# Re-ordering the tail of a fused transformer block: output projection, LayerNorm statistics and pending down tiles around the last attention group

## Chip, cores, metric

One core of one Trainium2 chip. The metric is the device time of one execution in microseconds (us), the median of several runs; a change of less than 2% counts as "same". Each run carries the granted TensorE clock; all runs used here were classed as fast. Each run is one core, so there is no second die to compare with.

## The reference, cut to what matters

```python
# S = 2048 tokens, D = 640, H = 32 heads of Dh = 20, one K/V head, Df = 1536, bf16
def _A_ref(x, wq, wk, wv, wo):                 # multi-query attention
    q = (x @ wq).reshape(B, S, H, Dh).transpose(0, 2, 1, 3)
    k, v = x @ wk, x @ wv
    p = softmax(einsum("bhqd,bkd->bhqk", q, k) * Dh ** -0.5)
    return einsum("bhqk,bkd->bhqd", p, v) ... @ wo
def _B_ref(x, w_gate, w_up, w_down):           # gated FFN
    return (gelu(x @ w_gate) * (x @ w_up)) @ w_down
h  = x + _A_ref(layernorm(x), ...)
h2 = h + _B_ref(layernorm(h), ...)
```

## The kernel before

The tokens are handled in four chunks of 512. In each chunk there are eight groups of four heads ("gi", 32 in all), and each group needs 16 steps of score matmul, exp on ScalarE, and value matmul. While attention of chunk 1, 2, 3 runs, TensorE's spare time takes the output projection, LayerNorm and FFN of the chunk before. So after the last exp a *tail* is left that nothing can hide: finish the last group, project chunk 3, normalise it, transpose it by DMA, its whole FFN (12 units), its four down tiles, and four *pending* down tiles of chunk 2. (A down tile is the last product of the FFN for 128 tokens: 12 matmuls of 512 columns, 12 of 128. `bank(n)` is one of eight accumulators in PSUM; TensorE fills it, and another engine has to read it before it is used again.)

Every operation is put in the queue of its engine in program order and waits for named events. In the traces here an operation late in a queue starts only behind the earlier ones of its engine, which is what this case is about. (An example, shown below: the matmuls for the first pending tile's first add end at 1033.2 us, and the add starts at 1040.08, behind the whole normalise.)

The last group is finished in a chain across VectorE ("dve") and TensorE ("pe"):

```python
def plan_group_copy(qc, g):       # after the last value matmul; bank(6) holds the sums
    plan.op("dve", ... tensor_copy(opvT32, bank(6)), mark=("ocopy", gi))
    plan.op("dve", ... tensor_copy(opvT16, opvT32), mark=("ocopy16", gi))
def piece_L(qc, g):               # broadcast each head's softmax sum over its rows
    plan.op("pe",  ... matmul(bank(7), bcast, opvT16), mark=("L", gi))
    plan.op("dve", ... tensor_copy(rL_sb, bank(7)), mark=("Lcopy", gi))
    plan.op("dve", ... reciprocal(rL_sb, rL_sb), mark=("recip", gi))
    plan.op("dve", ... onT[:, qc % 2, g, :] = opvT32 * rL_sb, mark=("onorm", gi))
```

The projection of a 128-token tile adds up eight head groups `g`; seven of them have been ready long before the last. The tail of the kernel before (shortened):

```python
piece_L(NQC - 1, NG - 1)()
def tail_wo(qc, qt):                       # two bank pairs (0,1), (2,3) in turn
    waits = [("onorm", gidx(qc, NG - 1)), ...] + S_FREE      # all eight groups wait
    plan.op("pe", lo_fn, wait=waits, mark=("wo_lo", t))      # 8 matmuls, columns 0..511
    plan.op("pe", hi_fn, wait=..., mark=("wo_hi", t))        # 8 matmuls, columns 512..639
    plan.op("dve", ... xh_sb += lo_b, mark=("attn_lo", t))
    plan.op("dve", ... xh_sb += hi_b, mark=("attn_hi", t))
for qt in range(TPC):
    tail_wo(NQC - 1, qt)
plan_ln2_chunk(NQC - 1)                    # all statistics, small chain, normalise, transposes
...
for tc in pending_down:                    # four tiles, bank pairs (4,5), (6,7) in turn
    for qt in range(TPC):
        ...                                # 12 + 12 matmuls, then fin_lo, fin_hi on dve
        if qt >= 2: waits6.append(("fin_lo", t - 2))
# then the FFN loop; its unit 0 waits for the last pending tiles' adds
```

In the FFN loop, per unit: `gu` (10 matmuls), `gs` (ScalarE copy), `sq`, `z` (VectorE), `th` (ScalarE tanh), `hg`, `hh` (VectorE): steps of gelu(gate) times up, and `hh` is the unit's result, which the down tiles read. VectorE's order in one iteration is hg and hh of unit i-2, z of i-1, sq of i.

The softmax here doesn't subtract the row's maximum and nothing guards it: scores larger than these inputs give would overflow.

## Time and profile before

| | before |
|---|---|
| median of 5 runs | 1108.76 us (1107.53 to 1110.01) |
| span of the profiled run | 1106.2 us |
| ScalarE busy | 89%, of it 950.9 us exp |
| tail, from the end of the last exp | 94.5 us |

From the page of the kernel before: span, line of busy times (busy us, share of the span, instructions), the chain by engine, and the costliest group of instructions.

```profile
span 1106.2 us, 13023 instructions
...
PE 755.6 (68%) x5424; PEld 203.1 (18%) x5508; DVE 461.5 (42%) x741; ACT 984.7 (89%) x1124; POOL 15.6 (1%) x20
...
ACT 63%; issue 17%; DVE 12%; PE 6%; DMA 1%; SPq 0%; POOL 0%; POOLq 0%
...
L485 ACT ACTIVATE scratch_a<-ps 128x1024 bf16<-128x1024 f32 x1024 | 950.9, 1138 | 23.8 <-PE ps L472 22.8
```

ScalarE's exp is the attention's limit and most of the chain. The change leaves all of that alone.

The timeline of the kernel before, in the tail: start us, length us, engine, line, operation, result<-inputs, shapes; in brackets the idle time of the engine just before and who ended it.

```profile
1012.42 0.69 DVE L519 COPY opvT<-ps 128x512 f32<-128x512 f32 x1 [19.09 <-PE ps L491]
...
1019.14 3.55 PE L978 MATMUL ps<-wo_pad,onT 128*128 128x512 bf16 x8 [6.77 <-DVE onT L541]
...
1022.72 0.69 DVE L993 TENSOR_TENSOR xh_sb<-xh_sb,ps 128x512 bf16<-128x512 bf16 x1 [3.64 <-PE ps L978]
...
1030.43 2.75 PE L786 MATMUL ps<-wd_sb,hhT 128*128 128x512 bf16 x12
...
1034.72 0.21 DVE L286 BATCH_NORM_AGGREGATE mv<-stats 128x2 f32<-128x12 f32 x1
...
1038.04 5.16 SPq L337 DMA_TRANSPOSE xnT<-xn_tmp  x4
...
1039.78 0.39 DVE L329 TENSOR_SCALAR xn_tmp<-xn_tmp,ln_r 128x640 bf16<-128x640 bf16 x1
1040.08 0.68 DVE L803 TENSOR_TENSOR xh_sb<-xh_sb,ps 128x512 bf16<-128x512 bf16 x1
...
1040.82 5.30 PE L786 MATMUL ps<-wd_sb,hhT 128*128 128x512 bf16 x12 [3.24 <-DVE xh_sb L803]
...
1051.04 0.78 PEld L682 LDWEIGHTS ps<-xnT,wg_sb 128*128 128x128 bf16 x5 [0.61 <-issue]
...
1087.29 0.69 DVE L741 SCALAR_TENSOR_TENSOR hhT<-g_th,ps 128x512 bf16<-128x512 bf16 x1
...
1088.03 4.10 PE L786 MATMUL ps<-wd_sb,hhT 128*128 128x512 bf16 x12 [5.80 <-DVE hhT L741]
```

How to read it. The last group's first copy starts at 1012.42; I use that moment as zero below, because all that comes before is attention. Until the last multiply is done TensorE has only the one broadcast matmul `L` (its record is missing, so the 6.77 us of idle time include it); it starts the projection at 1019.14. The last statistic starts at 1034.72, the transposes start at 1038.04 and take 5.16 us. The third pending tile starts at 1040.82, released by the first pending tile's add at 1040.08, which had stood behind the normalise (last step 1039.78) though its matmuls, started at 1030.43, had long ended. The third tile's 12 wide matmuls take 5.30 us, where the first tile's took 2.75. The first gate matmul's weights are loaded at 1051.04.

The granted clock (next to last but two) in stretches of the kernel before; columns: stretch, its length, then busy time and instructions of TensorE, its weight loads, VectorE, ScalarE, GpSimd, then clock, DMA share, GB/s.

```profile
1019.14:1021.00 1.86, 1.86 (x5) 0.73 (x6) 0.00 (x0) 0.00 (x0) 0.00 (x0) 0.50 0.00 0
1023.00:1026.00 3.00, 2.94 (x25) 1.55 (x23) 1.56 (x4) 0.00 (x0) 0.00 (x0) 1.00 0.00 0
...
1041.00:1044.00 3.00, 3.00 (x8) 1.06 (x7) 0.75 (x2) 0.00 (x0) 0.00 (x0) 0.50 0.68 132
1088.00:1090.00 2.00, 1.97 (x5) 0.73 (x6) 0.00 (x0) 0.00 (x0) 0.00 (x0) 0.50 0.00 0
```

Half clock after each long wait: at the projection's start, at the third pending tile, at the first of the last down tiles.

### The profile page before, as it was taken

To read this page: it belongs to the slowest core of one execution; us is meant where nothing else is said; L and a number is where in the kernel's file an instruction comes from. 1 tells how busy PE (TensorE), PEld (TensorE's weight loads), DVE (VectorE), ACT (ScalarE), POOL (GpSimd) and SP (SyncE) were. 2 spreads that over 40 slices of the span, in tenths; PEclk is the share of its full clock that TensorE was granted. 3 is DMA by queue.
4 is the path that set the end of the run, shared out by engine and by line. 5 is a ranking of instruction groups with operands and counts; after the bars stand their busy time and mean duration, and the time that the engine had idled before them with its cause. 6 is when DMAs were issued, how large, how long until landed. Compare 5 with 4: busy or idle time off the path is not lost.

```text
span 1106.2 us, 13023 instructions
## 1 busy us (share of the span) xinstructions
PE 755.6 (68%) x5424; PEld 203.1 (18%) x5508; DVE 461.5 (42%) x741; ACT 984.7 (89%) x1124; POOL 15.6 (1%) x20
## 2 busy tenths in 40 slices
PE   1677666666667776666876777667776776765886
PEld 0111111111121111111222111111221111111433
DVE  7433222111254666411224456661224356642574
ACT  3799999999899999999999999999999999995041
POOL 3000000000000000000000000000000000000000
PEclk9699655555899999755999999985999699985899
DMA  6360000000000000000000100000000100000100
GB/s 168 77 221 1 1 1 1 1 1 0 1 12 12 1 1 1 1 1 1 13 12 1 25 1 1 1 1 1 19 7 1 25 1 1 1 1 0 42 7 24
DMA packets 31819, 18.92 MB, mean 17 GB/s; under 512 B 23568, under 2 KB 30480, under 8 KB 31760
## 3 DMA queue, kind: packets, MB, share of 16 engines
q1 hardware_dynamic: 31760, 18.08, 6.0%
q8 instruction: 43, 0.70, 0.3%
q14 instruction: 16, 0.13, 0.0%
HBM read 10.21 MB, written 2.62 MB: 12 GB/s over the span
## 4 chain that ended last, share of the span: by engine, by line
ACT 63%; issue 17%; DVE 12%; PE 6%; DMA 1%; SPq 0%; POOL 0%; POOLq 0%
ACT scratch_a L485 61%; DVE rL_sb L537 3%; PE ps L786 2%; ACT g_th L728 2%; PE ps L682 1%; DVE hhT L741 1%; DVE g_th L733 1%; DVE g_sq L722 1%; DVE stats L281 1%; PE ps L491 1%; DVE stats L276 1%; PE ps L472 1%; DVE xn_tmp L329 1%; DMA xh_sb<-in_A_x_dram 1%; DVE xn_tmp L321 1%
## 5 line engine op out<-in xcount | busy, mean ns | idle before, releaser
L485 ACT ACTIVATE scratch_a<-ps 128x1024 bf16<-128x1024 f32 x1024 | 950.9, 1138 | 23.8 <-PE ps L472 22.8
L491 PE MATMUL ps<-scratch_a,v_ext 128*32 128x512 bf16 x2048 | 244.9, 469 | 194.1 <-ACT scratch_a L485 187.5
L472 PE MATMUL ps<-qT,kT 32*128 32x512 bf16 x2048 | 242.6, 464 | 85.9 <-ACT scratch_a L485 79.1
L491 PEld LDWEIGHTS ps<-scratch_a,v_ext 128*32 128x32 bf16 x2048 | 54.0, 96 | 383.4 <-ACT scratch_a L485 377.0
L519 DVE COPY opvT<-ps 128x512 f32<-128x512 f32 x32 | 22.1, 691 | 243.7 <-PE ps L491 243.7
L472 PEld LDWEIGHTS ps<-qT,kT 32*128 32x128 bf16 x2048 | 53.3, 94 | 313.1 <-ACT scratch_a L485 299.0
L537 DVE RECIPROCAL rL_sb<-rL_sb 128x512 f32<-128x512 f32 x32 | 107.3, 3353 | 1.1
L682 PE MATMUL ps<-xnT,wu_sb 128*128 128x512 bf16 x228 | 67.1, 399 | 7.7 <-DVE g_gs L710 5.7
L682 PE MATMUL ps<-xnT,wg_sb 128*128 128x512 bf16 x220 | 63.4, 390 | 9.4 <-DVE hhT L741 4.0
L786 PE MATMUL ps<-wd_sb,hhT 128*128 128x512 bf16 x185 | 52.2, 413 | 9.8 <-DVE hhT L741 5.8
L712 ACT ACTIVATE g_gs<-ps 128x512 bf16<-128x512 f32 x12 | 7.2, 597 | 54.8 <-PE ps L682 54.8
L775 DVE CAST g_us<-ps 128x512 bf16<-128x512 f32 x36 | 24.9, 690 | 74.4 <-PE ps L682 74.4
L535 DVE COPY rL_sb<-ps 128x512 f32<-128x512 f32 x32 | 22.0, 689 | 60.2 <-PE ps L491 53.2
L423 DVE CAST qT<-ps 128x512 bf16<-128x512 f32 x31 | 21.4, 690 | 56.7 <-PE ps L601 56.7
L710 DVE CAST g_gs<-ps 128x512 bf16<-128x512 f32 x36 | 24.8, 689 | 40.7 <-PE ps L682 40.7
L728 ACT ACTIVATE g_th<-g_sq 128x512 bf16<-128x512 bf16 x48 | 34.7, 724 | 5.4 <-DVE g_sq L722 5.4
L733 DVE SCALAR_TENSOR_TENSOR g_th<-g_th,g_gs 128x512 bf16<-128x512 bf16 x48 | 32.9, 686 | 6.8 <-ACT g_th L728 6.7
L722 DVE SCALAR_TENSOR_TENSOR g_sq<-g_sq,g_gs 128x512 bf16<-128x512 bf16 x48 | 32.7, 682 | 0.0
L626 PE MATMUL ps<-wo_pad,onT 128*128 128x512 bf16 x88 | 28.2, 395 | 4.9 <-DVE onT L541 3.6
L803 DVE TENSOR_TENSOR xh_sb<-xh_sb,ps 128x512 bf16<-128x512 bf16 x16 | 11.0, 685 | 44.4 <-PE ps L786 44.4
L633 DVE TENSOR_TENSOR xh_sb<-xh_sb,ps 128x512 bf16<-128x512 bf16 x12 | 8.2, 685 | 49.7 <-PE ps L626 49.7
L592 PE MATMUL ps<-xnT,wq_pad 128*128 128x512 bf16 x85 | 23.6, 382 | 5.1 <-DVE qT L423 4.3
(69 smaller groups left out, 363.6 us busy)
## 6 DMA issues: line engine op xcount, KB each, us to landing
out_dram<-xh_sb SPq DMA_DIRECT2D x16, 160.0 KB, 1.8
xh_sb<-in_A_x_dram SPq DMA_DIRECT2D x3, 640.0 KB, 8.5
wg_sb<-in_B_w_gate_dram SPq DMA_DIRECT2D x1, 1920.0 KB, 8.9
wu_sb<-in_B_w_up_dram SPq DMA_DIRECT2D x1, 1920.0 KB, 13.4
wd_sb<-in_B_w_down_dram SPq DMA_DIRECT2D x1, 1920.0 KB, 18.1
hhT<-in_A_wq_dram SPq DMA_DIRECT2D x1, 800.0 KB, 6.5
wo_pad<-in_A_wo_dram SPq DMA_DIRECT2D x32, 25.0 KB
xh_sb<-in_A_x_dram SPq DMA_DIRECT2D x4, 160.0 KB, 2.8
```

The lines of the kernel that those rows point to most:

```text
L472: ins = e.matmul(bank(PAIRS[pr][rr]), kT4[32 * r:32 * r + 32, kt * P:(kt + 1) * P], qT[32 * r:32 * r + 32, qc % 2, g, :], start=True, stop ...
L485: return e.activation(PT[s % 2][:, half * 1024:(half + 1) * 1024], src, ACT.Exp, scale=SM_SCALE)
L491: ins = e.matmul(ps[32 * hl:32 * hl + 32, 6 * 512:7 * 512], v_ext[:, kt, :], PT[s % 2][:, hl * 512:(hl + 1) * 512], start=(kt == 0), stop= ...
L537: plan.op("dve", (lambda e: e.reciprocal(rL_sb[:], rL_sb[:])), wait=[("Lcopy", gi)], mark=("recip", gi))
L626: ins = e.matmul(bank(7), onT[:, qc % 2, g, qt * P:(qt + 1) * P], wo_pad[:, g, 0:512], start=(g == 0), stop=(g == NG - 1))
L682: ins = e.matmul(bk, wsb[:, cc, fc * P:(fc + 1) * P], xnT[:, cc, tok], start=(cc == 0), stop=(cc == NC_D - 1))
L710: plan.op("dve", (lambda e: e.tensor_copy(g_gs[:, s3(k), :], src)), wait=waits, mark=("gs", k))
L722: plan.op("dve", (lambda e: e.scalar_tensor_tensor(g_sq[:, s2(k), :], g_sq[:, s2(k), :], GELU_K, g_gs[:, s3(k), :], ALU.add, ALU.mult)), w ...
L728: plan.op("act", (lambda e: e.activation(g_th[:, s2(k), :], g_sq[:, s2(k), :], ACT.Tanh, scale=GELU_C)), wait=[("z", k)] + ([("hh", kp)] i ...
L733: plan.op("dve", (lambda e: e.scalar_tensor_tensor(g_th[:, s2(k), :], g_th[:, s2(k), :], 1.0, g_gs[:, s3(k), :], ALU.add, ALU.mult)), wait ...
L775: plan.op("dve", (lambda e: e.tensor_copy(g_us[:, s2(k), :], bank(7))), wait=waits, mark=("us", k))
L786: ins = e.matmul(bk, hhT[:, tc % 2, fc, qt * P:(qt + 1) * P], wd_sb[:, fc, 0:512], start=(fc == 0), stop=(fc == NFC - 1))
```

## The change

Its intent: use TensorE's wait for the last group, start the normalise earlier on VectorE, and get pending down tiles out of the way of the FFN. No instruction is removed; the profile counts 5424 matmuls in both kernels. Its core:

```diff
-    piece_L(NQC - 1, NG - 1)()
...
-    for qt in range(TPC):
-        tail_wo(NQC - 1, qt)
-    plan_ln2_chunk(NQC - 1)
+    def tail_wo_all(qc):
...                            # every tile has its own bank pair (2*qt, 2*qt + 1)
+        def post(qt):          # the last head group alone, then adds and statistics of this tile
+            ...
+            plan.op("pe", fn, wait=[("onorm", gi_last)], mark=[("wo_lo", t), ("wo_hi", t)])
+            plan.op("dve", ... mark=("attn_lo", t)); plan.op("dve", ... mark=("attn_hi", t))
+            ln_stats(1, qc, ..., tiles=[t], chain=(qt == TPC - 1))
+        items = [(g, False) for g in range(NG - 1)] + [(g, True) for g in range(NG - 1)]
+        w0 = [("onorm", gi_last - 1), "dma_wo"] + S_FREE
+        pre(0, items[:3], "wo_pre0", w0)
+        piece_L(qc, NG - 1)()
+        pre(0, items[3:], "wo_pre", w0)
+        pre(1, items, "wo_pre", w0)
+        post(0)
+        post(1)
+        pre(2, items, "wo_pre", w0)
+        post(2)
+        pre(3, items, "wo_pre", w0 + [("ocopy", LAST_GI), ("Lcopy", LAST_GI)])
+        post(3)
...
-    for tc in pending_down:                       # four tiles, two bank pairs
+    for t in pd_tiles[:3]:                        # three tiles, three bank pairs
...
+            if it == NTU + 1:                     # the fourth, after the last gate/up matmuls
+                t = pd_tiles[3]
+                ...                               # banks 0 and 1, once hh of unit 9 is done
```

(The declarations, the wait lists and the adds of the down tiles are cut. FFN units 0, 1 and 2 each wait for the adds of one pending tile, where unit 0 had waited for all.)

More of the change, by code (lines that the diff above doesn't have):

```diff
@@ L962, in bass_sequential_preLN__grouped_kv_mqa__glu_gated_geglu__prompt_kernel @@
             fn()
-    piece_L(NQC - 1, NG - 1)()
     LAST_GI = gidx(NQC - 1, NG - 1)
     S_FREE = [("Ea", NS - 1), ("Eb", NS - 1), ("Ea", NS - 2), ("Eb", NS - 2), ("pv", NS - 1)]
-    def tail_wo(qc, qt):
-        t = qc * TPC + qt
-        lo_b = bank(2 * (qt % 2))
-        hi_b = bank(2 * (qt % 2) + 1)
-        waits = [("onorm", gidx(qc, NG - 1)), "dma_wo"] + S_FREE
-        if qt >= 2:
-            waits.append(("attn_lo", t - 2))
-        def lo_fn(e):
-            ins = None
-            for g in range(NG):
-                ins = e.matmul(lo_b, onT[:, qc % 2, g, qt * P:(qt + 1) * P], wo_pad[:, g, 0:512],
-                               start=(g == 0), stop=(g == NG - 1))
-            return ins
-        plan.op("pe", lo_fn, wait=waits, mark=("wo_lo", t))
-        waits = [("wo_lo", t)]
-        if qt >= 2:
-            waits.append(("attn_hi", t - 2))
-        def hi_fn(e):
-            ins = None
-            for g in range(NG):
-                ins = e.matmul(hi_b[:, 0:D - 512], onT[:, qc % 2, g, qt * P:(qt + 1) * P],
-                               wo_pad[:, g, 512:D], start=(g == 0), stop=(g == NG - 1))
-            return ins
-        plan.op("pe", hi_fn, wait=waits, mark=("wo_hi", t))
-        plan.op("dve", (lambda e: e.tensor_tensor(xh_sb[:, t, 0:512], xh_sb[:, t, 0:512], lo_b, ALU.add)),
-                wait=[("wo_lo", t), ("ln1", "norm", t)], mark=("attn_lo", t))
-        plan.op("dve", (lambda e: e.tensor_tensor(xh_sb[:, t, 512:D], xh_sb[:, t, 512:D], hi_b[:, 0:D - 512],
-                                                 ALU.add)),
-                wait=[("wo_hi", t)], mark=("attn_hi", t))
@@ L999, in bass_sequential_preLN__grouped_kv_mqa__glu_gated_geglu__prompt_kernel, with mm, pre, fn @@
-    for qt in range(TPC):
-        tail_wo(NQC - 1, qt)
-    plan_ln2_chunk(NQC - 1)
+    def tail_wo_all(qc):
+        gi_last = gidx(qc, NG - 1)
+        def mm(e, qt, g, hi):
+            t0 = qt * P
+            dst = bank(2 * qt + 1)[:, 0:D - 512] if hi else bank(2 * qt)
+            rhs = wo_pad[:, g, 512:D] if hi else wo_pad[:, g, 0:512]
+            return e.matmul(dst, onT[:, qc % 2, g, t0:t0 + P], rhs, start=(g == 0), stop=(g == NG - 1))
+        def pre(qt, items, tag, waits):
+            def fn(e):
+                for g, hi in items:
+                    ins = mm(e, qt, g, hi)
+                return ins
+            plan.op("pe", fn, wait=waits, mark=(tag, qt))
+        def post(qt):
+            t = qc * TPC + qt
+            def fn(e):
+                mm(e, qt, NG - 1, False)
+                return mm(e, qt, NG - 1, True)
+            plan.op("pe", fn, wait=[("onorm", gi_last)], mark=[("wo_lo", t), ("wo_hi", t)])
+            lo_b, hi_b = bank(2 * qt), bank(2 * qt + 1)
+            plan.op("dve", (lambda e: e.tensor_tensor(xh_sb[:, t, 0:512], xh_sb[:, t, 0:512], lo_b, ALU.add)),
+                    wait=[("wo_lo", t), ("ln1", "norm", t)], mark=("attn_lo", t))
+            plan.op("dve", (lambda e: e.tensor_tensor(xh_sb[:, t, 512:D], xh_sb[:, t, 512:D],
+                                                     hi_b[:, 0:D - 512], ALU.add)),
+                    wait=[("wo_hi", t)], mark=("attn_hi", t))
+            ln_stats(1, qc, lambda t: ("attn_hi", t), "ln2", tiles=[t], chain=(qt == TPC - 1))
+        items = [(g, False) for g in range(NG - 1)] + [(g, True) for g in range(NG - 1)]
[10 more added lines that the diff above has]
+        post(3)
@@ L1003, in bass_sequential_preLN__grouped_kv_mqa__glu_gated_geglu__prompt_kernel @@
+    tail_wo_all(NQC - 1)
+    WO_TAIL_DONE = [("attn_hi", NT - 1 - i) for i in range(TPC)] + [("attn_lo", NT - 1 - i) for i in range(TPC)]
+    ln_chain2(1, NQC - 1, "ln2")
+    ln_norm(1, NQC - 1, "ln2", ln2_xn_free)
     tail_units = [(tc, fc) for tc in range(NQC) if tc not in overlapped_ffn for fc in range(NFC)]
@@ L1013, in tail_gu @@
         waits = [("ln2", "T", tc), "dma_wg", "dma_wu"]
+        if i < 3:
+            waits += [("fin_lo", pd_tiles[i]), ("fin_hi", pd_tiles[i])]
         if i == 0:
-            waits += [("ocopy", LAST_GI), ("pv", NS - 1), ("attn_hi", NT - 1), ("attn_lo", NT - 1),
-                      ("attn_hi", NT - 2), ("attn_lo", NT - 2)] + S_FREE
-            for tcp in pending_down:
-                waits += [("fin_lo", tcp * TPC + TPC - 1), ("fin_hi", tcp * TPC + TPC - 1),
-                          ("fin_lo", tcp * TPC + TPC - 2), ("fin_hi", tcp * TPC + TPC - 2)]
+            waits += [("ocopy", LAST_GI), ("pv", NS - 1)] + S_FREE + WO_TAIL_DONE
         kp = kprev(k, 3)
@@ L1034, in tail_down_tile @@
     def tail_down_tile(t):
-        waits = [("hh", ffn_k(t // TPC, NFC - 1)), "dma_wd", ("ocopy", LAST_GI), ("pv", NS - 1)]
+        waits = [("hh", ffn_k(t // TPC, NFC - 1)), "dma_wd"]
         bank_acquire(6, waits)
@@ L1044, in tail_down_tile @@
         bank_release(7, ("fin_hi", t))
-    bank_free[7] = None
-    for tc in pending_down:
-        for qt in range(TPC):
-            t = tc * TPC + qt
-            lo_i, hi_i = (4, 5) if qt % 2 == 0 else (6, 7)
-            waits6 = [("hh", ffn_k(tc, NFC - 1)), "dma_wd", ("ocopy", LAST_GI), ("pv", NS - 1),
-                      ("recip", LAST_GI), ("Lcopy", LAST_GI)] + S_FREE
-            if qt >= 2:
-                waits6.append(("fin_lo", t - 2))
-            plan.op("pe", down_lo_fn(t, range(NFC), bank(lo_i)), wait=waits6, mark=("down_lo", t))
-            plan_fin_lo(t, bank(lo_i))
-            waits7 = [("down_lo", t)]
-            if qt >= 2:
-                waits7.append(("fin_hi", t - 2))
-            plan.op("pe", down_hi_fn(t, bank(hi_i)), wait=waits7, mark=("down_hi", t))
-            plan_fin_hi_out(t, bank(hi_i))
-        bank_free[6] = ("fin_lo", tc * TPC + TPC - 1)
-        bank_free[7] = ("fin_hi", tc * TPC + TPC - 1)
+    pd_tiles = [tc * TPC + qt for tc in pending_down for qt in range(TPC)]
+    assert len(pd_tiles) == TPC
+    for t in pd_tiles[:3]:
+        tc, qt = t // TPC, t % TPC
+        lo_i, hi_i = 2 * qt, 2 * qt + 1
+        waits6 = [("hh", ffn_k(tc, NFC - 1)), "dma_wd", ("attn_lo", NT - TPC + qt), ("attn_hi", NT - TPC + qt)]
+        plan.op("pe", down_lo_fn(t, range(NFC), bank(lo_i)), wait=waits6, mark=("down_lo", t))
+        plan_fin_lo(t, bank(lo_i))
+        plan.op("pe", down_hi_fn(t, bank(hi_i)), wait=[("down_lo", t)], mark=("down_hi", t))
+        plan_fin_hi_out(t, bank(hi_i))
+    bank_free[6] = ("attn_lo", NT - 1)
+    bank_free[7] = ("attn_hi", NT - 1)
     if NTU > 0:
@@ L1089, in bass_sequential_preLN__grouped_kv_mqa__glu_gated_geglu__prompt_kernel @@
                 plan_sq(ffn_k(*tail_units[i]), eng="dve")
+            if it == NTU + 1:
+                t = pd_tiles[3]
+                kf = ffn_k(*tail_units[9])
+                plan.op("pe", down_lo_fn(t, range(NFC), bank(0)),
+                        wait=[("hh", ffn_k(t // TPC, NFC - 1)), "dma_wd", ("hh", kf)], mark=("down_lo", t))
+                plan.op("pe", down_hi_fn(t, bank(1)), wait=[("down_lo", t)], mark=("down_hi", t))
+                plan_fin_lo(t, bank(0))
+                plan_fin_hi_out(t, bank(1))
             for t in down_queue.get(it, []):
```

## The prediction

> **What bounds the kernel now.** ScalarE is 89% busy and the exp activations (L485) are 61% of the chain of waits: about 950 us of attention. The change does not touch that. It touches only what follows the last exp (ends 1011.7 us in the timeline): a 94 us tail, which I read from the timeline and the waits from 1012 us:
> - 1012.4-1019.1: VectorE normalises the last group (copies, 3.35 us reciprocal, multiply). TensorE sits idle 6.8 us and its granted clock is 0.50.
> - 1019.1-1030.6: output projection, four tiles; the first 8 matmuls take 3.55 us cold, later eights 1.89.
> - 1030.8-1037.2: all LayerNorm statistics, then the small chain (about 2.3 us from the last aggregate to the first subtract), because every statistic is queued behind the last projection.
> - 1037.2-1044.5: normalise and four DMA transposes (1.28 us each one after another, 2.6 us to landing).
> - TensorE runs pending down tiles 1 and 2 meanwhile (3.55 us each), waits 3.2 us for VectorE (behind the normalise), cools to 0.50, runs tile 3 cold (6.1 us) and tile 4. The FFN starts only at 1051.3, though its transposes had landed by about 1044.5.
> - FFN 1051.3-1088.0: 2.71 us per unit, a VectorE/ScalarE loop.
> - Last down tiles 1088.0-1103.7, first one cold (4.1 against 2.76 us) after 5.8 us idle.
>
> **What the change does.**
> 1. Seven of eight heads-groups of projection tiles 0 and 1 (and all the low/high pieces) go before the last onorm, into the 6.8 us idle. This also warms the clock. The L matmul slips perhaps 0.1 us behind three cold matmuls (3 x 0.43 us). The last group of tile 0 then costs one 512- and one 128-column matmul: first add at about 1019.7 instead of 1022.7.
> 2. Statistics interleave with the adds: about 1.85 us VectorE per tile (0.6 add, 0.2 add, 1.05 statistics). Last aggregate near 1026.9 instead of 1034.7. TensorE delivers tile 3 at about 1024.7, before VectorE wants it (1025.2), so VectorE is the limit. First normalised tile 1030.2 (was 1038.0), transposes landed about 1036.7.
> 3. Three pending down tiles, warm and without bank waits, run 1024.5-1035.2 beside this; their adds finish about 1035.4.
> 4. The FFN starts near 1036.8, limited by the transposes, 14.5 us earlier. The loop itself keeps 2.71 us per unit.
> 5. The fourth pending tile (3.55 us) fits in the 5.8 us TensorE gap before the last down tiles, free, and keeps the clock warm: another 1.4 us.
>
> No instruction is removed; everything gained is idle or cold time on the critical chain. Sum: 14.5 + 1.4 = about 16 us, 1.4%.
>
> **Clock.** The Trainium skill, "TensorE: Matmul & The Clock Gate", Part 1, says the clock is half rate until about 3.4 us of sustained activity. The trace agrees: 3.55 us cold at 1019.1, full after. So I expect 1.00 from about 1016-1017.
>
> **Prediction: 1093 us, range 1090.5 to 1097.** Faster by over 2%: 0.02; within 2%: 0.97; slower: 0.01.
>
> **What would show it.** Projection matmuls between 1012.4 and 1019; first projection add at 1019.7; granted clock 1.00 from about 1017 to the end; the first gate matmul at about 1037, released by the transposes; the unit period still 2.71 us; down tile 4 between the last gate/up matmul and the last hh; first final down tile 2.76 us; the first 1011 us unchanged.
>
> **What would make it wrong.** The clock staying at half rate until 1019 or later (loses 1-2 us); early matmuls delaying L; 1.6-1.9 us idle gaps before the FFN or the last tiles cooling the clock again (1.4 us each); output DMAs delaying the transposes; a disturbed start of the FFN loop while adds share VectorE.

## The result, and the profile after

| | before | after |
|---|---|---|
| median | 1108.93 us (16 runs) | 1094.25 us (9 runs) |
| ratio | | 0.9871, 95% interval 0.9858 to 0.9884 |
| span of the profiled run | 1106.2 us | 1092.2 us |

A ratio is the mean time of one kernel's fast runs over that of the other's in the same rounds, so it is not quite the ratio of the medians quoted. The change gains 1.3%, 14.7 us of the medians, which counts as "same" at 2%.

The timeline of the kernel after, the lines that answer to those above:

```profile
1013.52 0.69 DVE L519 COPY opvT<-ps 128x512 f32<-128x512 f32 x1 [19.09 <-PE ps L491]
...
1014.01 1.06 PE L973 MATMUL ps<-wo_pad,onT 128*128 128x512 bf16 x2 [0.54 <-PE ps L491]
...
1020.40 5.06 PE L973 MATMUL ps<-wo_pad,onT 128*128 128x512 bf16 x35 [1.04 <-DVE onT L541]
1020.88 0.69 DVE L990 TENSOR_TENSOR xh_sb<-xh_sb,ps 128x512 bf16<-128x512 bf16 x1 [0.54 <-PE ps L973]
...
1028.46 0.21 DVE L286 BATCH_NORM_AGGREGATE mv<-stats 128x2 f32<-128x12 f32 x1
...
1031.78 5.16 SPq L337 DMA_TRANSPOSE xnT<-xn_tmp  x4
...
1038.33 0.76 PEld L682 LDWEIGHTS ps<-xnT,wg_sb 128*128 128x128 bf16 x5 [2.56 <-DMA xnT<-xn_tmp]
...
1069.89 2.76 PE L786 MATMUL ps<-wd_sb,hhT 128*128 128x512 bf16 x12 [0.38 <-DVE hhT L741]
...
1074.57 0.69 DVE L741 SCALAR_TENSOR_TENSOR hhT<-g_th,ps 128x512 bf16<-128x512 bf16 x1
...
1075.31 2.76 PE L786 MATMUL ps<-wd_sb,hhT 128*128 128x512 bf16 x12 [1.76 <-DVE hhT L741]
```

Zero is now 1013.52. TensorE starts projecting 0.1 us after it (the first matmul record is missing; its weights are loaded at 1013.60). The first add comes at 1020.88, the last statistic at 1028.46, the transposes at 1031.78, the first gate weights at 1038.33, released by the transposes (DMA xnT). The fourth pending tile runs at 1069.89, in the wait for the last hh, and the first of the last down tiles takes 2.76 us, not 4.10.

The clock of the kernel after, stretches as before:

```profile
1012.90:1015.30 2.40, 1.86 (x8) 0.60 (x10) 1.12 (x2) 0.00 (x0) 0.00 (x0) 0.50 0.00 0
1015.30:1017.30 2.00, 2.00 (x13) 0.98 (x12) 1.73 (x2) 0.00 (x0) 0.00 (x0) 0.63 0.00 0
1017.30:1020.30 3.00, 2.06 (x17) 1.06 (x14) 2.97 (x2) 0.00 (x0) 0.00 (x0) 1.00 0.00 0
1035.93:1038.33 2.40, 0.02 (x1) 0.00 (x0) 0.36 (x2) 0.00 (x0) 0.00 (x0) 1.00 0.68 136
...
1075.30:1077.30 2.00, 1.99 (x10) 0.92 (x11) 0.75 (x2) 0.00 (x0) 0.00 (x0) 1.00 0.18 65
```

Half clock for the first 3.2 us of early projection (from 1013.60 to 1016.80), then full, also through the 2.4 us wait before the FFN.

The same milestones from zero, for all profiled runs (each of one execution). "Last statistic" is the start of the last aggregate. "Middle" is from the first gate weights to the start of the last hh, "end part" from there to the end of the span.

| run | last statistic | transposes start | FFN starts | middle | end part | end |
|---|---|---|---|---|---|---|
| before | 22.30 | 25.62 | 38.62 | 36.25 | 18.91 | 93.78 |
| after | 14.94 | 18.26 | 24.81 | 36.24 | 17.63 | 78.68 |
| e12 (after again) | 14.94 | 18.27 | 24.83 | 36.24 | 17.64 | 78.71 |
| e1 warm only | 20.99 | 24.31 | 36.31 | 36.24 | 19.99 | 92.54 |
| e5 down tiles only | 23.29 | 26.61 | 33.18 | 37.71 | 17.61 | 88.50 |
| e6 projection and statistics only | 14.94 | 18.26 | 28.63 | 36.24 | 19.96 | 84.83 |
| e3 after, projection late | 20.17 | 23.49 | 30.05 | 36.22 | 17.62 | 83.89 |
| e2 after, statistics last | 16.67 | 19.99 | 26.58 | 37.91 | 17.56 | 82.05 |
| e10 e2 kept warm | 16.68 | 20.00 | 26.55 | 36.24 | 17.61 | 80.40 |
| e4 after, tile 4 early | 14.94 | 18.26 | 25.71 | 36.27 | 19.62 | 81.60 |
| e7 after, FFN loop | 14.93 | 18.25 | 24.81 | 30.66 | 17.61 | 73.08 |
| e8 e7 and a shorter head | 13.59 | 16.91 | 23.48 | 32.26 | 17.62 | 73.36 |
| e11 e8, tile 4 split | 13.60 | 16.92 | 23.50 | 30.67 | 17.55 | 71.72 |

The tail gained 93.78 - 78.68 = 15.1 us: 13.8 at the FFN's start, 1.3 in the end part, nothing in the middle. Zero itself lies between 1011.95 and 1015.22 in these profiles without a clear pattern by kernel (1013.52 and 1012.99 for the change in two runs), so 1 or 2 us of the whole time are the attention's own scatter. The tail repeats to 0.03 us between the two profiles of the change, so I argue with tails and give the timed ratios beside them.

### The profile page after: what moved, and what is told of

Read it like the earlier page. It is cut to its first block, busy times and chain, and to the rows that moved or that the text cites. A ratio compares the mean times of both kernels' runs of the same rounds, so it can differ in the third digit from the quotient of the medians.

```text
span 1092.2 us, 13019 instructions
## 1 busy us (share of the span) xinstructions
PE 753.7 (69%) x5424; PEld 202.5 (19%) x5508; DVE 460.9 (42%) x741; ACT 984.8 (90%) x1124; POOL 15.6 (1%) x20
## 4 chain that ended last, share of the span: by engine, by line
ACT 63%; issue 17%; DVE 12%; PE 6%; DMA 1%; SPq 0%; POOL 0%; POOLq 0%
ACT scratch_a L485 62%; DVE rL_sb L537 3%; ACT g_th L728 2%; PE ps L682 1%; PE ps L786 1%; DVE hhT L741 1%; DVE g_th L733 1%; PE ps L472 1%; PE ps L491 1%; DVE g_sq L722 1%; DVE stats L281 1%; DVE stats L276 1%; DVE xn_tmp L329 1%; DVE xn_tmp L321 1%; DMA xh_sb<-in_A_x_dram 1%
## 5 line engine op out<-in xcount | busy, mean ns | idle before, releaser
L786 PE MATMUL ps<-wd_sb,hhT 128*128 128x512 bf16 x185 | 48.1, 388 | 2.9 <-DVE hhT L741 2.1
L733 DVE SCALAR_TENSOR_TENSOR g_th<-g_th,g_gs 128x512 bf16<-128x512 bf16 x48 | 32.9, 686 | 6.8 <-ACT g_th L728 6.7
L722 DVE SCALAR_TENSOR_TENSOR g_sq<-g_sq,g_gs 128x512 bf16<-128x512 bf16 x48 | 32.7, 682 | 0.0
```

The source lines that it names most:

```text
L722: plan.op("dve", (lambda e: e.scalar_tensor_tensor(g_sq[:, s2(k), :], g_sq[:, s2(k), :], GELU_K, g_gs[:, s3(k), :], ALU.add, ALU.mult)), w ...
L733: plan.op("dve", (lambda e: e.scalar_tensor_tensor(g_th[:, s2(k), :], g_th[:, s2(k), :], 1.0, g_gs[:, s3(k), :], ALU.add, ALU.mult)), wait ...
L786: ins = e.matmul(bk, hhT[:, tc % 2, fc, qt * P:(qt + 1) * P], wd_sb[:, fc, 0:512], start=(fc == 0), stop=(fc == NFC - 1))
```

## The experiments

**Theory (two chains).** Two chains meet where the FFN starts: VectorE's (last multiply, adds, statistics, normalise, then DMA transposes) and TensorE's (projection, then pending tiles, waiting for VectorE to empty their banks). The FFN starts at the later. The change shortens both, and gains 1.3 us at the end by keeping TensorE warm. **Rivals:** the gain is the clock (TensorE is kept warm); it is the down tiles alone; it is projection and LayerNorm alone.

All runs below were correct. Each was timed in five rounds against the kernel before (4 to 6 executions).

### e1: the clock alone

```diff
 (before)  piece_L(NQC - 1, NG - 1)()
+    for _ in range(14):     # on pe, after L; bank 0 is overwritten later by the projection
+        e.matmul(bank(0), onT[:, (NQC - 1) % 2, 0, 0:P], wo_pad[:, 0, 0:512], start=True, stop=True)
```

> The kernel before, with 14 extra 128x512 matmuls into a free bank (their result is overwritten) in TensorE's idle time before the last normalise; nothing else moves. Times from the start of the last group's first copy: before, FFN starts at +38.65 us and the span ends at +93.8. Two-chains theory (both chains that meet at the FFN start have to be shortened, the clock is a small part): the first projection tile runs warm, 1.95 instead of 3.6 us, so everything after comes about 1.6 us earlier: FFN at +37.0, end at +92.2, ratio about 0.9985. Clock theory (the change gains because TensorE is kept warm): most of the 15 us, at least 8: end below +86.

Measured: 1106.60 us, ratio 0.9983 (0.9968 to 0.9999). The FFN started at +36.31, 2.3 us earlier, but the end came only 1.2 us earlier. Of the 2.3 us the first projection tile gives 1.3 (first add at +8.99, before +10.30; 1.6 were expected), and 0.9 come from the third pending tile, which was cold for a shorter time (4.39 us, before 5.30), while the first of the last down tiles was cold for longer (5.17, before 4.10). I read these two as scatter of the clock (see e10). e1 warms only the first of three cold stretches; but all three together lose 5.6 us in the kernel before (3.55 against 1.89, 5.30 against 2.75, 4.10 against 2.76). So the clock is real, and as the whole cause of a 15 us gain it is ruled out.

### e5: the down tiles alone

```diff
 (before)
-    for tc in pending_down: ...                 # four tiles, bank pairs (4,5), (6,7)
+    DB = [(4, 5), (6, 7), (0, 1)]
+    for t in pd_tiles[:3]: ...                  # three tiles, three bank pairs
...
+            if it == NTU + 1: ...               # the fourth in the last gap, as in the change
```

> The kernel before with only the pending down tiles re-placed as in the change (three before the FFN without bank waits, the fourth in the gap before the last down tiles); projection and statistics as before. Two-chains theory: the FFN start is now set by the transposes, which stay where they were: FFN at about +32.2 us, 6.4 earlier than before; the end another 1.3 earlier: +86.1 (up to 1.2 later if the 3.5 us wait cools the clock), ratio about 0.993. If the down tiles are the whole gain: end at +78.7. If the projection and LayerNorm part is the whole gain: end near +92.5.

Measured: 1102.23 us, ratio 0.9937 (0.9917 to 0.9957). FFN at +33.18, end at +88.50. The timeline of e5 at the start of the FFN:

```profile
1039.91 5.18 SPq L337 DMA_TRANSPOSE xnT<-xn_tmp  x4
...
1042.09 0.84 PE L797 MATMUL ps<-wd_sb,hhT 128*128 128x128 bf16 x12
...
1046.49 2.32 PE L682 MATMUL ps<-xnT,wg_sb 128*128 128x512 bf16 x5 [3.56 <-DMA xnT<-xn_tmp]
```

TensorE is done with the pending tiles at 1042.9 and waits 3.56 us for the transposes, so the other chain now sets the start, as the theory says. The start was 1.0 us later than expected, because the first projection tiles ran at half clock for longer (last statistic at +23.29, in the kernel before +22.30). The first gate and up matmuls are cold (the first five take 2.32 us; in e6 below, warm, 1.24), which cost 1.5 us in the middle: the loss the expectation had allowed up to 1.2 for.

### e6: projection and statistics alone

```diff
 (after)
-    for t in pd_tiles[:3]: ...                  # and the fourth in the last gap
+    for tc in pending_down: ...                 # as before: four tiles, bank pairs (4,5), (6,7)
+            else: waits6 += [("attn_lo", NT - 2 + qt), ("attn_hi", NT - 2 + qt)]   # banks free
```

> The change's early projection and interleaved statistics, with the four pending down tiles in two bank pairs before the FFN as in the kernel before. Two-chains theory: transposes land at +24.8 us as in the change, but the FFN is held by the adds of the fourth down tile: tile 3 waits for VectorE behind the normalise, FFN at about +28.9 us, last down tiles start cold, end at about +84.1, ratio about 0.991. If this part is the whole gain: end at +78.7. If the down tiles are the whole gain: end near +92.

Measured: 1099.81 us, ratio 0.9921 (0.9905 to 0.9936). Transposes start at +18.26 exactly as in the change, yet the FFN starts at +28.63. The timeline of e6, TensorE alone:

```profile
1035.50 2.76 PE L786 MATMUL ps<-wd_sb,hhT 128*128 128x512 bf16 x12 [1.74 <-DVE xh_sb L803]
...
1043.13 1.24 PE L682 MATMUL ps<-xnT,wg_sb 128*128 128x512 bf16 x5 [0.47 <-DVE xh_sb L807]
```

The third pending tile waits 1.74 us for an add that stands behind the normalise on VectorE, and the gate matmul is released by the fourth tile's add, not by the transposes. So neither half is the whole.

How the 13.8 us at the FFN start split depends on the order in which one counts: down tiles first gives 5.4 (38.62 to 33.18), then 8.4 for the rest; projection and statistics first gives 10.0 (38.62 to 28.63), then 3.8. That is what a maximum of two chains does: "the share" of one part is not a number.

### e3: projection late

```diff
 (after)
-        pre(0, items[:3], "wo_pre0", w0)
         piece_L(qc, NG - 1)()
-        pre(0, items[3:], "wo_pre", w0); pre(1, items, "wo_pre", w0); post(0); post(1)
+        w0 = w0 + [("onorm", gi_last)]
+        pre(0, items, "wo_pre", w0); post(0); pre(1, items, "wo_pre", w0); post(1)
```

> The change with all projection matmuls behind the last normalise again (tile by tile), the rest kept. Two-chains theory: first add at about +10.2 us instead of +7.4, TensorE then feeds a tile every 2.4 us and the last one is late, the last add starts at +17.5 instead of +13.2, so transposes and FFN come 4.4 us later: FFN at +29.2, end at +83.1, ratio about 0.991. If early projection only buys the warm clock: 1.7 us later, end at +80.4.

Measured: 1098.59 us, ratio 0.9909 (0.9893 to 0.9925); FFN at +30.05, end at +83.89. The first add in e3's timeline:

```profile
1025.41 0.69 DVE L990 TENSOR_TENSOR xh_sb<-xh_sb,ps 128x512 bf16<-128x512 bf16 x1 [4.54 <-PE ps L973]
```

Without the early start the change loses 5.2 us, 0.8 more than expected (the first add came at +11.20 instead of +10.2: a longer cold start again, 5.6 us). The warm clock alone would have been 1.7. The early matmuls matter because they leave two matmuls, not sixteen, between the last multiply and the first add, and because TensorE then stays ahead: in the change VectorE's adds and statistics follow each other without a gap, in e3 the adds wait for TensorE (+11.20, +13.98, +16.16, +18.33).

### e2 and e10: statistics last, and the same kept warm

```diff
 (after)   def post(qt):
-            ln_stats(1, qc, ..., tiles=[t], chain=(qt == TPC - 1))
 ...
     tail_wo_all(NQC - 1)
+    ln_stats(1, NQC - 1, ..., "ln2")
```

> The change with the four tiles' statistics again after the fourth tile's adds instead of between them; the rest kept. Times from the start of the last group's first copy; the change has its last aggregate at +14.9 us, FFN at +24.8, end at +78.7. Two-chains theory: the last adds end at about +12.7, then four statistics of 1.0 us each: last aggregate at about +16.5, FFN at +26.4, end at +80.3, ratio to the kernel before about 0.988 to 0.989. If the interleaving is the main part of the LayerNorm gain (the aggregate was at +22.3 in the kernel before): aggregate at +19 or later, end above +82.5.

Measured: 1095.83 us, ratio 0.9890 (0.9867 to 0.9914). The last statistic moved to +16.67 and the FFN to +26.58, as expected, but the end was +82.05 and not +80.3. The middle had grown from 36.24 to 37.91. e10 tests whether that is the clock:

```diff
 (e2)
+    for _ in range(16):     # on pe, before the FFN, into free bank 6 (not used until later)
+        e.matmul(bank(6), onT[:, (NQC - 1) % 2, 0, 0:P], wo_pad[:, 0, 0:512], start=True, stop=True)
```

> e2 (statistics last) with 16 extra matmuls into a free bank in TensorE's 4.3 us of waiting before the FFN; their result is overwritten. e2 ended at +82.05 us where +80.3 was expected, though its FFN started as expected (+26.58). If the missing 1.7 us is the clock, which fell to half rate for the first 4 us of the FFN: the granted clock stays 1.00, the time from the first gate matmul to the last hh falls from 37.9 us to the 36.2 that the change has, end at +80.3. If it is something else in the late statistics: 37.9 again, end at +82.

Measured: FFN at +26.55, middle 36.24, end +80.40; 1096.20 us, ratio 0.9891 (0.9872 to 0.9910). Clock by stretches in e2, with the start of the FFN at the second line (columns as above):

```profile
1036.13:1038.53 2.40, 0.00 (x0) 0.00 (x0) 0.32 (x2) 0.00 (x0) 0.00 (x0) 1.00 0.67 138
1038.53:1040.53 2.00, 2.00 (x6) 0.76 (x7) 0.00 (x0) 0.00 (x0) 0.00 (x0) 0.64 0.59 209
1040.53:1042.53 2.00, 2.00 (x6) 0.76 (x5) 0.00 (x0) 0.00 (x1) 0.00 (x0) 0.51 0.00 0
```

The same stretches, counted from the FFN's start, of e10:

```profile
1038.15:1040.55 2.40, 1.68 (x8) 0.59 (x6) 0.36 (x2) 0.00 (x0) 0.00 (x0) 1.00 0.67 135
1040.55:1042.55 2.00, 2.00 (x10) 0.94 (x11) 0.00 (x0) 0.00 (x0) 0.00 (x0) 1.00 0.62 216
1042.55:1044.55 2.00, 2.00 (x11) 0.93 (x10) 0.96 (x2) 0.60 (x1) 0.00 (x0) 1.00 0.04 8
```

The clock it is: 0.64 and 0.51 became 1.00, and 1.7 us came back in the profile. In the timed runs the two kernels are not apart (0.9890 and 0.9891, each interval about 2 us to either side, too wide to see 1.7 us), so the profiled executions show the mechanism and its size, not a gain one can bank on.

That executions meet the clock differently can be read from the clock records in the kept traces. In each of the 13 profiles all changes of the granted clock lie whole multiples of 3.413 us apart, and this grid lies differently in each execution: with the same instructions up to there, the clock rose 3.2 us after the first early weights in the change, 3.4 in e12, and 5.4 in e4, e6 and e10.

The interleaving itself is worth 1.8 us at the FFN start, a small part of the 7.4 us by which the statistics moved.

### e4: the fourth pending tile before the FFN

```diff
 (after)
-    for t in pd_tiles[:3]:
+    for t in pd_tiles:
-            if it == NTU + 1: ...
```

> The change with the fourth pending down tile before the FFN as well (in the banks of the fourth projection tile). Two-chains theory: TensorE is then the later of the two chains, FFN at +26.0 us (1.2 later), and the last down tiles start cold after an idle gap of 5.8 us, 1.3 to 2.4 later: end at +81.2 to +82.3, ratio about 0.989. If the fourth tile's 3.55 us are fully exposed before the FFN: FFN at +28.4. If it is hidden and only the clock counts: FFN at +24.8, end at +80.

Measured: 1096.31 us, ratio 0.9894 (0.9872 to 0.9917). FFN at +25.71, 0.9 later; end part 19.62, 2.0 longer (first of the last tiles 4.82 us); end +81.60. The tile fits nearly for free into the wait for the transposes; its move to the last gap pays mostly (2.0 of 2.9 us) by keeping TensorE warm there.

### e7, e8, e11: what the traces point to next

The middle stood at 36.24 us in every warm run with the change's loop, and its chain of waits is a cycle: tanh, hg, hh, z. In the kernel after VectorE's order puts z of the next unit behind hh of the last. e7 breaks the cycle:

```diff
 (after)   tail_gu:
-        plan.op("pe", fn, wait=waits, mark=[("gmm", k), ("umm", k)])
+        plan.op("pe", fn_g, wait=waits, mark=("gmm", k)); plan.op("pe", fn_u, mark=("umm", k))
 ... loop:
+            tail_sq(i)                       # ScalarE: activation(g_sq, g_gs, ACT.Square)
+            plan_z(i - 1)                    # now ahead of hg and hh
             plan_hg(i - 2); plan_hh(i - 2)
-            plan_z(i - 1)
             plan_th(i - 1)
-            plan_sq(i, eng="dve")
```

> The change, with the FFN loop taken up too, which the change left at 2.71 us per unit: the square goes to ScalarE, z is placed before hg and hh on VectorE, and the gate half signals by itself. If the loop's period is the cycle tanh, hg, hh, z (0.64 + 0.70 + 0.69 + 0.61 and waits = 2.71) as the chain of waits shows: it falls to TensorE's time for ten matmuls, about 2.2 to 2.3 us, the last hh comes about 5 us earlier, end at +73.5 to +75, ratio about 0.982 to 0.983. If the loop is bound by VectorE's busy time (2.42 before, 2.00 now) the same period results; if by the banks (hh to the gate matmul three units on): period stays above 2.6 and the end above +77.5.

Measured: 1089.19 us, ratio 0.9825 (0.9803 to 0.9847). Middle 30.66 us, end +73.08. Timeline of VectorE; L741 is hh, L722 z, L733 hg. First the kernel after:

```profile
1058.30 0.69 DVE L741 SCALAR_TENSOR_TENSOR hhT<-g_th,ps 128x512 bf16<-128x512 bf16 x1
...
1060.28 0.69 DVE L733 SCALAR_TENSOR_TENSOR g_th<-g_th,g_gs 128x512 bf16<-128x512 bf16 x1 [0.36 <-ACT g_th L728]
1061.01 0.69 DVE L741 SCALAR_TENSOR_TENSOR hhT<-g_th,ps 128x512 bf16<-128x512 bf16 x1
```

The same view of e7:

```profile
1060.06 0.69 DVE L741 SCALAR_TENSOR_TENSOR hhT<-g_th,ps 128x512 bf16<-128x512 bf16 x1
1060.89 0.69 DVE L722 SCALAR_TENSOR_TENSOR g_sq<-g_sq,g_gs 128x512 bf16<-128x512 bf16 x1
1061.51 0.68 DVE L733 SCALAR_TENSOR_TENSOR g_th<-g_th,g_gs 128x512 bf16<-128x512 bf16 x1
1062.22 0.69 DVE L741 SCALAR_TENSOR_TENSOR hhT<-g_th,ps 128x512 bf16<-128x512 bf16 x1
...
1064.72 0.69 DVE L741 SCALAR_TENSOR_TENSOR hhT<-g_th,ps 128x512 bf16<-128x512 bf16 x1
```

In the kernel after hg waits 0.36 us for the tanh in every steady unit and hh follows hh by 2.71 us. In e7 the period alternates between 2.16 and 2.50, mean 2.33, and TensorE is now busy for 4.50 of every 4.66 us, nearly the limit itself. VectorE's busy time in the old loop is 2.32 us per unit in the profile (not 2.42, as the expectation had it), and 1.98 in e7. Without the 0.36 us wait the old loop would take 2.35 us per unit, by my estimate, so breaking the cycle alone might have given most of the gain; but e7 changed three things at once, and which of them is worth what is not tested.

e8 also shortens the first steps of the tail, for the last group alone:

```diff
 (e7)
+            plan.op("dve", ... tensor_copy(opvT16, bank(6)), mark=("ocopy16", gi))   # first
+            plan.op("dve", ... tensor_copy(opvT32, bank(6)), mark=("ocopy", gi))
 ...
-            tensor_copy(rL_sb, bank(7)); reciprocal(rL_sb, rL_sb)
+            reciprocal(rL_sb, bank(7))
 ...                                      # one early matmul instead of three ahead of L;
                                          # tile 1's seven narrow ones go behind post(0)
```

> e7 and the first steps of the tail shortened for the last group alone: the bf16 copy is made first and straight from PSUM, the reciprocal reads PSUM and the copy before it falls away. Two-chains theory: VectorE is the limit from the last exp to the transposes, so the reciprocal starts at about +1.45 us instead of +2.74, and FFN comes 1.0 to 1.3 us earlier (+23.6 to +23.8), end 1.0 to 1.3 before that of e7, ratio about 0.981. If TensorE's early matmuls become the limit: less than 0.5 us.

Measured: 1087.75 us, ratio 0.9814 (0.9792 to 0.9837). FFN at +23.48, 1.33 us earlier as expected, but in the profiled run the end was 0.3 *later* than e7's, because the FFN started at half clock (middle 32.26). The wait in e8 and the start of its FFN:

```profile
1034.30:1036.12 1.82, 0.00 (x0) 0.00 (x1) 0.14 (x1) 0.00 (x0) 0.00 (x0) 0.97 0.61 130
1036.12:1036.60 0.48, 0.48 (x2) 0.20 (x3) 0.00 (x0) 0.00 (x0) 0.00 (x0) 0.50 1.00 352
```

e11 fills that wait with useful work:

```diff
 (e8)
+    plan.op("pe", down_lo_fn(t3, range(0, 8), bank(6)), ...)     # before the FFN
 ...
-                plan.op("pe", down_lo_fn(t, range(NFC), bank(0)), ...)
+                plan.op("pe", down_lo_fn(t, range(8, NFC), bank(6)), ...)   # the rest in the last gap
 ...                                      # the first of the last tiles moves to banks 2 and 3
```

> e8 with the fourth pending down tile split: 8 of its 512-column matmuls in TensorE's wait before the FFN, the rest in the gap before the last down tiles. In e8's trace the FFN started at half clock after 2.2 us of waiting. If that start is a clock loss: warm start, first gate to last hh falls from 32.3 us to 30.7, end at about +71.8 (e8 +73.4, e7 +73.1), ratio to the kernel before about 0.979 to 0.981. If not: end at +73.4, ratio 0.981.

Measured: middle 30.67, end +71.72, the shortest tail of all; 1087.65 us, ratio 0.9814 (0.9794 to 0.9833). In the timed runs it can't be told from e8. Both beat the kernel before and the change; against e7 the intervals of both overlap.

### e12: the change again

> The change itself again, unaltered, on the chip of these runs. All theories: ratio to the kernel before 0.986 to 0.988; tail +78.7 us when the FFN starts warm, up to 1.7 us more[...].

Measured: 1094.64 us, ratio 0.9877 (0.9856 to 0.9897), tail 78.71.

## Why the prediction was right

It said 1093 us, 1090.5 to 1097; measured were 1094.25. Point by point, from zero:

- *Early projection and first add*: predicted 7.3 us after zero (1019.7), measured 7.36. The broadcast matmul's copy slipped by 0.16 us (predicted "perhaps 0.1"). e3 shows that the early projection is worth 5.2 us, of which some 0.8 are e3's longer cold start.
- *Interleaved statistics, VectorE the limit*: predicted 1.85 us per tile, measured 1.93 on average (adds at +7.36, +9.33, +11.24, +13.15). The last statistic was predicted at 14.5 after zero and came at 14.94. Right in kind, 0.46 us short: these small terms, summed over four tiles, are over half of what the sum missed.
- *FFN start, limited by the transposes*: predicted, and the trace names the DMA as the releaser. "14.5 us earlier" measured 13.8. The other part of the miss: I counted the old start at the first recorded matmul (1051.3), whose neighbour was missing from the trace; its weights were loaded at 1051.04.
- *Loop unchanged at 2.71 us per unit*: measured 2.71, middle 36.25 and 36.24.
- *Fourth tile free in the last gap, "another 1.4 us"*: measured 1.28 (end part 18.91 to 17.63).
- *Clock 1.00 from about 1016-1017*: it rose at 1016.80. The prediction took the warm-up time of about 3.4 us from the Trainium skill, "TensorE: Matmul & The Clock Gate", Part 1, and this trace agrees with 3.2 us. That it came so soon was luck: in e4 and e6 the same early projection took 5.4 us to warm up. It would not have mattered, for their last statistic came at +14.94 all the same.
- *Idle time before the FFN*: predicted 1.6 us with a risk of cooling, measured 2.39 us. The clock held in all three profiles with this wait (the change, e7, e12), but e8 lost it in a wait of 2.0 us, so I count that as partly luck too.
- *"The first 1011 us unchanged"*: the same instructions, but the last group's copy came 1.1 us later in the profile after, 0.6 in e12. This is scatter of the attention part; its origin was not tested.

Tail 15.1 against the predicted 15.9; medians 14.7. The mechanism was the predicted one, and the sizes missed by 0.8 us.

## What to carry to other kernels

Where a stage waits for two chains, find both and shorten both: half of the change would have left the start to the other one (e5, e6), and shares of the gain depend on the order of counting. In an in-order queue ask of each operation what it stands behind: partial sums that need not wait for the last input, statistics behind all the adds, adds behind a normalise. Time a tail from its own first instruction rather than from the start of the program, and look at the granted clock at each restart before blaming a change for a microsecond or two.

## What the Trainium skill lacked or had wrong

- "TensorE: Matmul & The Clock Gate", Part 1 (What's actually happening), gives about 3.4 us of idleness for the clock to fall and says that the windows run free. The grid of 3.413 us that lies differently in each execution (e10) agrees with windows that run free, but less idleness was enough: after a wait of 2.0 us (e8) the clock was at 0.50 from the next matmuls on, after 2.4 us (the change, e7, e12) it stayed at 1.00. In e2 it still read 1.00 through a wait of 4.16 us and fell 0.55 us after work had *resumed* (mean 0.64, then 0.51). The page does not say outright how little idleness is enough, nor that the fall can come after the wait is over; a restart cost 1.5 to 1.7 us in the middle part here.
- "DMA: Bandwidth & Descriptors", Latency and other measured facts, gives 261 GB/s for DMA transposes with a non-contiguous middle dimension in one kernel, and no time per small transpose; no page has one for this size. Here four transposes of 128x640 bf16 in a row took 1.28 us each on the queue, which works out at 163,840 bytes / 1.28 us = 128 GB/s, with 2.6 us from issue to landing; that latency sits in full on the critical path (last issue at 1035.7, first gate weights at 1038.33).
